# Pooling additions and half of the quarter sums on GpSimd, and attention spread anew over two blocks

## The chip, the cores and the metric

The kernel runs on one core of one Trainium2 chip. The metric is the device time of one execution in microseconds (us), from the start of the program on the core to its end; lower is better. Five engines work side by side, each through its own queue in order: TensorE (PE in the profile; its weight loads are PEld), VectorE (DVE), ScalarE (ACT), GpSimd (POOL) and SyncE (SP), which here only starts transfers. An engine whose next instruction waits for something does nothing else meanwhile.

## The reference

```python
# attention over pooled keys and values: 8 batches, 8 heads, 576 tokens, head size 64, pool 8
k_p = k.reshape(B, H, 72, 8, D).mean(axis=3)
v_p = v.reshape(B, H, 72, 8, D).mean(axis=3)
scores = scale * np.matmul(q, k_p.transpose(0, 1, 3, 2))
attn = softmax(scores)                       # max subtracted, sum + 1e-9
x = np.matmul(attn, v_p)                     # -> (4608, 512)
# the feed-forward part
h = x @ w_in                                 # (512, 2048)
g = h * np.clip(h + 3.0, 0.0, 6.0) / 6.0
out = g @ w_out                              # (2048, 512)
```

All is in float32. The kernel gets near that by splitting each factor of a large product into a rounded part and a remainder and making three products (rounded by rounded, rounded by remainder, remainder by rounded).

## The kernel before

**Blocks.** The 4608 tokens are cut into blocks of 512, 256, 384 and 384 tokens and then eight of 384. The first four are worked plainly. The last eight are taken in four pairs of 768 tokens, called super blocks below, numbers 0 to 3. In each, the feed-forward products are made by a fast scheme with seven products in place of eight (kinds 1 to 7): the four quarters of a factor are added to and subtracted from each other before and after.

**A super block** has two parts. The h part (`super_block`) makes h from x and the weights in 112 steps (products at L1134), adds kept results (L1098), applies the gate on ScalarE (L1090) and VectorE (L1092), and leaves g, whose quarters lie side by side in one tile per pair. The output part multiplies g by w_out. In super block 0 it is plain (`out_plain`, L1188), in 1 to 3 it goes by the seven kinds (`out_seven`, products at L1261). There, 28 steps follow each other, kinds in the order 1, 2, 4, 5, 6, 7, 3, four steps (m = 0 to 3) to a kind; each step has 18 products of 256 columns. Before each step a quarter of g is split by `split_g` into its rounded part (ScalarE, L1113) and the remainder (VectorE, L1115); there are three buffers for such parts, and a part is made two steps ahead. After the split for kind 1, `mix` makes quarter 0 minus 2 into 0 and 2 plus 3 into 2; after that for kind 4, 3 minus 0 into 3 and 1 minus 3 into 1 (L1218). A mix is an addition or subtraction of 128 x 768 numbers. The splits and mixes of m = 0, 1 and 2 for kind 1 already run during the h part.

**Attention for the next pair** is woven between the products of a super block by a pacer (`Paced`): so many steps per slot. A step is the scores of one 128-token tile for four heads (product, maximum on VectorE, four exponentials on ScalarE, sum and reciprocal on VectorE, and two products `a` and `ar` on GpSimd, L501 and L507), or the transposes of `a` (L572, L574) with the split of their result (L583, L585, L596, L598), or a product with the values (L646). `CUTS` says which share of a pair's attention steps goes to the h part of super blocks 0 to 3; the rest is spread over the first 48 of the 84 slots of the output part (in `out_plain`, over 66 slots), before x is combined for the next super block.

**Pooled values.** For each batch, `load_v` brings the values in ten transfers into ring buffers named vst (six of them, vr_l, for the last 8 pooled rows of each head), four buffers being shared with other tiles. `prep_v` then makes, three times per batch, three additions of halving width (512, 256 and 128 columns, L383) on VectorE, in place. `place_heads` (L395, L396) and `place_rest` (L409, L410) scale the sums, split them and put them into block-diagonal tiles `vhi`, `vlo` and `vrem`, the factors of the product with the values. At the first of them GpSimd clears two tiles (L374), which waits until the batch before last is no longer read.

**Order.** Up to some point in block 1 the order on each queue is written out by hand (`ORDER`). After it, a planner orders the instructions by its own estimates of their times. `after_mark` adds an edge that puts an instruction behind the last marked one of the same engine; marks are made for VectorE, ScalarE, and SyncE instructions of the feed-forward part, and for none of GpSimd's.

Of the kernel before, what the change touches and what calls it, by code (L numbers as in the profile page):

```python
# [13 lines left out]
ALU = mybir.AluOpType  # L14
# [31 lines left out]
SEVEN = (1, 2, 3)  # L46
MAKE = (range(8), (), (), ())
TURN = (0, 2, 4, 6, 7, 9, 10, 12)
CUTS = (.85, 0.85, 0.85, 0)
TAIL = 5  # L50
WSCALE = 2.0**8
GSCALE = WSCALE**-2
# [46 lines left out]
def attention_moe_kernel(  # L99
# [19 lines left out]
    nc = tc.nc  # L119
# [46 lines left out]
    def behind(ins, name):  # L166
        no_sync = mybir.DependencyInfo(mybir.DependencyClass.NoSync, mybir.DependencyReason.DATA)
        tc.add_manual_dep(ins, name, no_sync, reason="order")
# [14 lines left out]
    def after_mark():  # L183

        if len(window) == 2 and traced[-1].engine in marks:
            behind(traced[-1], marks[traced[-1].engine])
# [141 lines left out]
    class FirstValues:  # L328
# [19 lines left out]
        def place_heads(self):  # L348
            for h in range(2):
                rows = slice(h * D, (h + 1) * D)  # L350
                nc.scalar.mul(self.v32[rows, :, h * D : (h + 1) * D], self.ps[rows], 1.0 / POOL)
# [14 lines left out]
    def place_v(b):  # L366

        W[b] = (
            pool.tile([P, NPAIR, 2 * D], F32R, name="vhi", bufs=2),
            pool.tile([P, NPAIR, 2 * D], F32R, name="vlo", bufs=2),  # L370
            pool.tile([3 * REM, NG, 4 * D], F32R, name="vrem", bufs=2),
        )
        for w in W[b][:2]:
            nc.gpsimd.memset(w.bitcast(F32), 0.0)  # L374

    def prep_v(b, p):

        if p == 0 and b not in W:
            place_v(b)
        n = P if p < NPAIR else 3 * REM  # L380
        x, y = (vraw.pop((b, p + i))[:n, : POOL * D].rearrange("p (c n) -> p c n", c=2) for i in range(2))
        for w, a, c in ((4 * D, x, y), (2 * D, x, x[:, :, 2 * D :]), (D, x, x[:, :, D:])):
            nc.vector.tensor_tensor(out=x[:, :, :w], in0=a[:, :, :w], in1=c[:, :, :w], op=ALU.add)  # L383
            after_mark()
        if p < NPAIR:
            place_heads(b, x[:, :, :D], slice(p, p + 2))
        else:
            place_rest(b, x[:, :, :D])
# [16 lines left out]
    def place_rest(b, vs):  # L405
        lo = slice(REM, 2 * REM)
        for h in range(4):
            to, own = W[b][2][:, :, h * D : (h + 1) * D], mask[:NR, 2 + h : 3 + h]
            nc.scalar.mul(to, vs[:NR], own)  # L409
            nc.vector.scalar_tensor_tensor(  # L410
                out=to[lo],
                in0=vs[lo],
                scalar=own[lo],
                in1=to[lo].bitcast(F32),
                op0=ALU.mult,
                op1=ALU.subtract,
            )
# [238 lines left out]
    def side_steps(b):  # L656

        ks = [lambda p=p: load_k(b, p) for p in range(NPAIR)]
        ks += [lambda p=p: prep_k(b, p) for p in range(NPAIR)]
        vs = []  # L660
        n = NPAIR + NG
        for p in range(n):
            vs.append(lambda p=p: load_v(b, p))
            if p > 2 and p % 2:
                vs.append(lambda p=p: prep_v(b, p - 3))
        vs.append(lambda: prep_v(b, n - 2))
        return ks, vs
# [336 lines left out]
    def next_w2(n, x):  # L1004
        return chunk(first_of[n] + len(w_dram) + x).rearrange("p (k m c) -> p k m c", k=2, m=2)
# [198 lines left out]
    def out_seven(n, j, bank, parts, split_g, split_f, pairs, att, rest, last_h):  # L1204
        NT2, NM, W2 = HALF // P, NF // 4, DM // 2
        todo = [(o, m) for o in KINDS for m in range(NM)]
        n_tail = NT2 * 12
        paced, last = Paced(att, len(todo) * NT2 - n_tail), Paced([([], x) for x in rest], n_tail - NT2)
        rest.clear()
        sets = {"X": ["o2", "o1"], "Z": ["o0", "o3"], "V": ["h1", "h0"], "Y": ["o0", "o3"]}  # L1210
        on = {2: "Z", 1: "X", 4: "V", 5: "Y", 6: "X", 7: "X", 3: "Y"}
        first = (1, 2, 4, 5)
        src = {2: 1, 1: 0, 4: 3, 5: 2, 6: 3, 7: 0, 3: 1}
        ps, kept, made = {}, {}, [0]

        def mix(m, to, a, b, how):
            g = pairs[m]
            nc.vector.tensor_tensor(out=g[:, :, to], in0=g[:, :, a], in1=g[:, :, b], op=how)  # L1218

        def upto(x):  # L1220
            while made[0] <= x and made[0] < len(todo):
                o, m = todo[made[0]]
                split_g((o, m), pairs[m][:, :, src[o]])
                made[0] += 1
                if o == 1:
                    mix(m, 0, 0, 2, ALU.subtract)
                    mix(m, 2, 2, 3, ALU.add)
                elif o == 4:
                    mix(m, 3, 3, 0, ALU.subtract)
                    mix(m, 1, 1, 3, ALU.subtract)  # L1230

        def to_sbuf(o):
            c = late[1].tile([P, 2, HALF], F32, name="kept", tag="c", bufs=NC)
            kept[o] = c.rearrange("p a b -> p (a b)")
            for x, (lo, hi) in enumerate(((0, 2 * W2), (2 * W2, 3 * W2))):
                nc.scalar.copy(kept[o][:, lo:hi], ps[on[o]][x])

        def result(o, half, q, name):
            for x, (t0, t1) in enumerate(((0, 2), (2, 3))):
                c = kept[o][:, t0 * W2 : t1 * W2]  # L1240
                nc.vector.tensor_tensor(out=c, in0=ps[name][x], in1=c, op=ALU.add)
                at = starts[j] + half * HALF
                rows = out[at + t0 * P : at + t1 * P, q * W2 : (q + 1) * W2]
                nc.sync.dma_start(rows.rearrange("(t p) c -> p t c", p=P), c.rearrange("p (t c) -> p t c", c=W2))

        for x, (o, m) in enumerate(todo):
            upto(x + 2)
            w, t = next_w2(n, x), parts[o, m]
            name = on[o]
            if m == 0 and o in first:  # L1250
                ps[name] = [bank(sets[name], 0, 2 * W2), bank(sets[name], 1, W2)]
            for i in range(NT2):
                if x * NT2 + i < len(todo) * NT2 - n_tail:
                    paced.slot()
                else:
                    last.slot()
                to = ps[name][i // 2][:, i % 2 * W2 : (i % 2 + 1) * W2]
                begin = o in first and m == 0
                for k in range(2):
                    for y, (l, r) in enumerate(((0, 0), (0, 1), (1, 0))):  # L1260
                        nc.tensor.matmul(  # L1261
                            to,
                            t[:, l, k, i * P : (i + 1) * P],
                            w[:, k, r],
                            start=begin and k == 0 and y == 0 and i % 2 == 0,
                            stop=m == NM - 1 and k == 1 and y == 2,
                            skip_group_check=True,
                        )
                        if begin and k == 0 and y == 0:
                            behind(traced[-1], last_h if i % 2 == 0 else opened)  # L1270
                            opened = traced[-1].name
            if x * NT2 + NT2 >= len(todo) * NT2 - n_tail:
                paced.upto(len(paced.steps))
            if m < NM - 1:
                continue
            if o in (1, 4, 5, 6):
                to_sbuf(o)
            if o == 2:
                result(1, 0, 0, "Z")
            elif o == 7:  # L1280
                result(5, 1, 1, "X")
                result(4, 1, 0, "X")
            elif o == 3:
                result(6, 0, 1, "Y")
# [18 lines left out]
    a = [Step(first, f, 0, 2) for f in range(SPLIT)]  # L1303
# [33 lines left out]
    b = [Scores(t, g) for g in range(NG) for t in B]  # L1337
# [66 lines left out]
    def att_steps(j):  # L1404

        if j == 1:
            ks, _ = side_steps(1)
            return [([x], None) for x in ks[NPAIR:]] + [x[:2] for x in block_steps(1)]
        return [x[:2] for x in later_steps[j]]
# [106 lines left out]
    for n, j in enumerate(supers):  # L1516
        last = n == len(supers) - 1
        att = [] if last else att_steps(j + 2) + att_steps(j + 3)
        cut = int(CUTS[n] * len(att))
        super_block(n, j, att[:cut], att[cut:])  # L1520
# [46 lines left out]
```

## Time and profile before

| | us |
|---|---|
| median of three runs | 893.63 (892.76 to 893.68) |
| the profiled execution | 893.88 |
| its span in the profile | 892.1 |
| TensorE busy | 869.2 (97%) |
| VectorE busy | 665.9 (75%) |
| ScalarE busy | 553.6 (62%) |
| GpSimd busy | 83.6 (9%) |

The span is the time from the first to the last instruction of the execution. Places in it are given in us from its start. The super blocks lie at about 346 to 494 (output part from 423), 494 to 633 (from 566), 633 to 769 (from 704) and 769 to the end (from 828). A row of groups gives the line, the engine, the operation, what is written from what, the shapes and the count, then the busy time in us and the mean of one in ns, then the idle time before them and what ended it. A row of a time line gives start and length in us and, in brackets, the idle time before it and what ended that. The product time of TensorE is partly modelled: consecutive products overlap in the record.

### The profile page before, as it was taken

How to read it: one execution, taken by the hardware profiler on the slowest of the kernel's cores; microseconds unless marked ns; L12 is line 12 of the kernel's file. 1: busy time of each engine (PE TensorE's matmuls, PEld its weight loads, DVE VectorE, ACT ScalarE, POOL GpSimd, SP SyncE). 2: the span in 40 equal slices, each digit the busy share in tenths (PEclk: the TensorE clock that was granted, in tenths of full speed). 3: DMA queues.
4: the chain of work that ended last, by engine and by line, in shares of the span. 5: the costliest groups of instructions: out<-in, count | busy, mean ns of one | idle time of the engine just before them, and what ended most of it. 6: DMA issues, size and time to landing. Idle time of an engine off the chain costs nothing.

```text
span 892.1 us, 15646 instructions
## 1 busy us (share of the span) xinstructions
PE 869.2 (97%) x5360; PEld 812.3 (91%) x5360; DVE 665.9 (75%) x1340; ACT 553.6 (62%) x1515; POOL 83.6 (9%) x168
## 2 busy tenths in 40 slices
PE   7899999999999999999999999999999999999998
PEld 6788888988989998998888999999999999999998
DVE  6999864567877785869788688897597877466664
ACT  5998766655656655778344688665577746355442
POOL 4100002110211100102000101100100200000000
PEclk9999999999999999999999999999999999999999
DMA  9970205995425234996587968877976777877873
GB/s 294 392 293 1 72 24 192 360 327 167 130 67 160 71 129 135 368 315 225 180 271 239 383 218 295 265 239 236 331 250 213 226 233 240 275 253 238 266 264 132
DMA packets 124654, 200.00 MB, mean 224 GB/s; under 512 B 13216, under 2 KB 81056, under 8 KB 124576
## 3 DMA queue, kind: packets, MB, share of 16 engines
q1 hardware_dynamic: 124432, 199.00, 67.8%
q8 instruction: 43, 0.70, 0.3%
q14 instruction: 35, 0.29, 0.1%
q10 hardware_dynamic: 144, 0.00, 0.0%
HBM read 158.08 MB, written 40.89 MB: 223 GB/s over the span
## 4 chain that ended last, share of the span: by engine, by line
PE 80%; DVE 8%; DMA 5%; ACT 4%; issue 2%; SPq 1%; POOL 0%; DVEq 0%; ACTq 0%; POOLq 0%
PE psx L1134 22%; PE psx L1261 19%; PE pso L872 12%; PE psh L841 12%; PE psx L1188 7%; PE psa L646 3%; PE psa L463 3%; ACT e L472 2%; PE psa L572 1%; DMA raw<-w_in_l 1%; DMA raw<-w_out_l 1%; DMA wd<-wq 1%; DVE vst L383 1%; DMA wsFalse<-wd 1%; DVE wq L939 1%
## 5 line engine op out<-in xcount | busy, mean ns | idle before, releaser
L1134 PE MATMUL psx<-x,wsFalse 128*128 128x384 f32 x768 | 151.8, 341 | 1.7 <-DVE g L1098 0.8
L841 PE MATMUL psh<-xhi,w 128*128 128x384 f32 (+2 forms) x520 | 145.9, 340 | 0.5 <-DVE g L853 0.4
L1134 PEld LDWEIGHTS psx<-x,wsFalse 128*128 128x128 f32 x768 | 133.6, 188 | 3.2 <-ACT c L1107 1.3
L1113 ACT CAST part<-g 128x768 fp32r<-128x768 f32 x100 | 83.3, 836 | 85.0 <-PE psx L1261 65.8
L1115 DVE TENSOR_TENSOR part<-g,part 128x768 fp32r<-128x768 f32 x100 | 95.2, 955 | 46.5 <-ACT part L1113 46.1
L872 PE MATMUL pso<-w,ghi 128*128 128x512 f32 x384 | 120.7, 398 | 0.4 <-ACT o L877 0.4
L1134 PE MATMUL psx<-x,wsTrue 128*128 128x384 f32 x576 | 115.8, 342 | 2.4 <-DMA wsTrue<-wd 2.3
L1261 PE MATMUL psx<-wsFalse,part 128*128 128x256 f32 x864 | 108.3, 282 | 1.5 <-DVE part L1115 1.1
L1261 PEld LDWEIGHTS psx<-wsFalse,part 128*128 128x128 f32 x864 | 105.2, 189 | 2.3 <-DVE part L1115 1.3
L1134 PEld LDWEIGHTS psx<-x,wsTrue 128*128 128x128 f32 x576 | 99.6, 188 | 3.1 <-DVE g L1092 3.1
L841 PEld LDWEIGHTS psh<-xhi,w 128*128 128x128 f32 x520 | 93.2, 188 | 8.2 <-DVE g L853 1.1
L472 ACT ACTIVATE e<-psa,mx 128x72 f32<-128x72 f32 x256 | 78.6, 324 | 23.7 <-DVE mx L467 22.4
L841 PE MATMUL psh<-xlo,w 128*128 128x384 f32 (+2 forms) x260 | 87.1, 336 | 0.0
L501 POOL TENSOR_TENSOR a<-e,sm 128x256 f32<-128x256 f32 x60 | 41.0, 683 | 478.3 <-DVE sm L490 377.9
L1261 PE MATMUL psx<-wsTrue,part 128*128 128x256 f32 x648 | 81.3, 283 | 0.0
L1261 PEld LDWEIGHTS psx<-wsTrue,part 128*128 128x128 f32 x648 | 79.3, 191 | 0.2 <-DVE part L1115 0.2
L872 PEld LDWEIGHTS pso<-w,ghi 128*128 128x128 f32 x384 | 69.1, 188 | 11.2 <-ACT o L877 0.7
L1090 ACT ACTIVATE r<-g,small 128x384 f32<-128x384 f32 x96 | 58.8, 621 | 28.4 <-DVE g L1098 28.0
L872 PE MATMUL pso<-w,glo 128*128 128x512 f32 x192 | 74.4, 399 | 0.0
L1098 DVE TENSOR_TENSOR g<-psx,c 128x384 f32<-128x384 f32 x96 | 52.3, 553 | 28.7 <-PE psx L1134 20.6
L1107 ACT COPY c<-psx 128x384 f32<-128x384 f32 x96 | 45.0, 485 | 28.5 <-PE psx L1134 28.1
L1092 DVE SCALAR_TENSOR_TENSOR g<-r,g 128x384 f32<-128x384 f32 x96 | 54.5, 576 | 9.7 <-ACT r L1090 9.2
(139 smaller groups left out, 1473.2 us busy)
## 6 DMA issues: line engine op xcount, KB each, us to landing
wsFalse<-wd SPq DMA_DIRECT2D x64, 512.0 KB, 4.6
wsTrue<-wd SPq DMA_DIRECT2D x48, 512.0 KB, 4.9
wsFalse<-w2d SPq DMA_DIRECT2D x31, 512.0 KB, 5.0
wsFalse<-w2t SPq DMA_DIRECT2D x27, 512.0 KB, 5.0
wsTrue<-w2d SPq DMA_DIRECT2D x21, 512.0 KB, 5.0
wsTrue<-w2t SPq DMA_DIRECT2D x21, 512.0 KB, 4.9
raw<-w_in_l SPq DMA_DIRECT2D x16, 512.0 KB, 8.6
raw<-w_out_l SPq DMA_DIRECT2D x16, 512.0 KB, 9.2
```

Of the source, the lines that this page charges most:

```text
L472: nc.scalar.activation(self.e[:, h], self.ps[:, h], AF.Exp, bias=self.mx[:, h : h + 1], accum_out=self.sm[:, h : h + 1])
L841: nc.tensor.matmul(self.ps, l[f][:, c, :], r[:, c, :], start=c == 0 and i == 0, stop=c == NCC - 1 and i == 2)
L872: nc.tensor.matmul(pos, l, r, start=f == 0 and i == 0, stop=f == NF - 1 and i == 2)
L1090: nc.scalar.activation(r, src, AF.Relu, bias=half_low, scale=GSCALE / (6.0 * WSCALE))
L1092: nc.vector.scalar_tensor_tensor(out=g_of[i][:, k], in0=r, scalar=GSCALE, in1=src, op0=ALU.min, op1=ALU.mult)
L1098: nc.vector.tensor_tensor(out=g_of[i][:, k], in0=ps, in1=kept, op=ALU.add)
L1107: nc.scalar.copy(c, ps)
L1113: nc.scalar.copy(t[:, 0], src)
L1115: nc.vector.tensor_tensor(out=t[:, 1], in0=src, in1=t[:, 0].bitcast(F32), op=ALU.subtract)
L1134: nc.tensor.matmul(ps, w[:, l, c * P : (c + 1) * P], t[:, r, c], start=o in (1, 2, 5) and c == 0 and k == 0, stop=c == 1 and k == 2, skip_ ...
L1188: nc.tensor.matmul(to, l, w[:, qs, r], start=f == 0 and k == 0, stop=end and k == 2)
L1261: nc.tensor.matmul(to, t[:, l, k, i * P : (i + 1) * P], w[:, k, r], start=begin and k == 0 and y == 0 and i % 2 == 0, stop=m == NM - 1 and ...
```

## The change

The three additions of `prep_v` go to GpSimd for batches 3 to 7 (batches 1 and 2 lie before or in the stretch ordered by hand, or use another function). `after_mark` is still called after each, but since GpSimd has no mark, it adds no edge. In `out_seven`, the mixes into quarters 1 and 2 go to GpSimd, those into 0 and 3 stay on VectorE. `CUTS` puts 65% in place of 85% of the next pair's attention into the h parts of super blocks 1 and 2, and so 35% in place of 15% into their output parts.

```diff
-CUTS = (.85, 0.85, 0.85, 0)
+CUTS = (.85, .65, .65, 0)
...
         for w, a, c in ((4 * D, x, y), (2 * D, x, x[:, :, 2 * D :]), (D, x, x[:, :, D:])):
-            nc.vector.tensor_tensor(out=x[:, :, :w], in0=a[:, :, :w], in1=c[:, :, :w], op=ALU.add)
+            engine = nc.gpsimd if b > 2 else nc.vector
+            engine.tensor_tensor(out=x[:, :, :w], in0=a[:, :, :w], in1=c[:, :, :w], op=ALU.add)
             after_mark()
...
         def mix(m, to, a, b, how):
             g = pairs[m]
-            nc.vector.tensor_tensor(out=g[:, :, to], in0=g[:, :, a], in1=g[:, :, b], op=how)
+            engine = nc.gpsimd if to in (1, 2) else nc.vector
+            engine.tensor_tensor(out=g[:, :, to], in0=g[:, :, a], in1=g[:, :, b], op=how)
```

## The prediction

> **What bounds the kernel now.** I read the page first: the busy shares and the chain that ended last.
>
> ```profile
> span 892.1 us, 15646 instructions
> PE 869.2 (97%) x5360; PEld 812.3 (91%) x5360; DVE 665.9 (75%) x1340; ACT 553.6 (62%) x1515; POOL 83.6 (9%) x168
> PE 80%; DVE 8%; DMA 5%; ACT 4%; issue 2%; SPq 1%; POOL 0%; DVEq 0%; ACTq 0%; POOLq 0%
> ```
>
> TensorE is the bound: it is busy 97% and carries 80% of the chain. The change takes no product away, so all that it can win is time in which PE stands still for another engine. VectorE's 8% of the chain is the candidate. The span is 892.1; the profiled execution took 893.88, so 1.8 us lie around the span, and it stands 0.25 above the median of the three runs, 893.63.
>
> Next, busy time in chosen stretches: length of the stretch, then busy time (instructions) of PE, PEld, DVE, ACT, POOL. I take the super blocks alone: of the moved work only batch 3's nine additions lie before them.
>
> ```profile
> 361.00:400.00 39.00, 39.00 (x236) 38.86 (x235) 32.30 (x77) 30.07 (x97) 4.16 (x10) 1.00 1.01 347
> 400.00:424.00 24.00, 22.69 (x139) 21.51 (x139) 20.75 (x58) 20.53 (x82) 6.16 (x11) 1.00 0.69 220
> 545.00:585.00 40.00, 37.81 (x259) 36.14 (x259) 34.98 (x75) 28.21 (x82) 5.62 (x12) 1.00 0.82 265
> 695.00:708.00 13.00, 12.41 (x86) 11.85 (x85) 10.82 (x30) 10.44 (x40) 3.99 (x8) 1.00 0.68 215
> 828.00:888.00 60.00, 60.00 (x504) 59.83 (x504) 36.70 (x45) 25.04 (x35) 0.00 (x0) 1.00 0.68 227
> ```
>
> PE is without work for 1.31 us at the end of the first 768-token block's h part, for 2.19 us where the second block passes from h to its output part, for 0.59 us at that place of the third block; in the stretches between, such as the first and the last row here, it is full. DVE is at 83 to 87% in just those three. The granted clock is 1.00 throughout. Then who PE waited for (total, times, longest), from the waits after 270 us (the one for the first weight chunk, near 356, is left out, since no edit touches it):
>
> ```profile
> PE psa L463 <- DVE arem L598: 1.3, 3, 0.9
> PE psx L1261 <- DVE part L1115: 1.1, 1, 1.1
> PE psx L1134 <- DVE g L1098: 0.8, 1, 0.8
> ```
>
> All three are DVE results, 3.2 of the 4.1 us. The time lines of PE and of DVE at two of these places say why DVE is late:
>
> ```profile
> 416.48 0.69 DVE L383 TENSOR_TENSOR vst<-vst 96x512 f32<-96x512 f32 x1 [0.81 <-DMA vst<-vr_l]
> ...
> 572.31 0.69 DVE L383 TENSOR_TENSOR vst<-vst 96x512 f32<-96x512 f32 x1 [3.57 <-DMA vst<-vr_l]
> ...
> 417.74 0.76 PE L463 MATMUL psa<-kbd,qt 128*128 128x144 f32 x4 [0.90 <-DVE arem L598]
> ...
> 581.63 2.04 PE L1261 MATMUL psx<-wsFalse,part 128*128 128x256 f32 x15 [1.07 <-DVE part L1115]
> ```
>
> The pooling add stands at the head of DVE's queue and waits for its values, 0.81 and 3.57 us, with everything else of DVE behind it; PE's 0.90 us pause ends 1.3 us after the first of these adds starts, its 1.07 us pause 9.3 us after the second.
>
> **The change part by part.** The groups concerned (busy us, mean ns, idle before):
>
> ```profile
> L383 DVE TENSOR_TENSOR vst<-vst 128x512 f32<-128x512 f32 (+5 forms) x54 | 26.2, 486 | 4.7 <-DMA vst<-vr_l 4.4
> L1218 DVE TENSOR_TENSOR g<-g 128x768 f32<-128x768 f32 x48 | 45.4, 953 | 0.4
> L1115 DVE TENSOR_TENSOR part<-g,part 128x768 fp32r<-128x768 f32 x100 | 95.2, 955 | 46.5 <-ACT part L1113 46.1
> L357 POOL TENSOR_TENSOR stage<-stage 32x512 f32<-32x512 f32 x1 | 1.3, 1252 | 8.1 <-DMA stage<-vr_l 8.1
> L357 POOL TENSOR_TENSOR stage<-stage 32x256 f32<-32x256 f32 x1 | 0.7, 715 | 0.1
> L501 POOL TENSOR_TENSOR a<-e,sm 128x256 f32<-128x256 f32 x60 | 41.0, 683 | 478.3 <-DVE sm L490 377.9 <-ACT e L472 30.5 <-ACT wq L945 22.6
> ```
>
> *Off DVE.* Six batches make the 54 adds; five of them (3 to 7) move, 45 x 0.486 = 21.9 us. Two of four mixes per pair move, 24 x 0.953 = 22.9 us. Together 44.8 of 665.9 us.
>
> *Onto POOL.* POOL's own two-tensor adds took 1.252 and 0.715 us: 0.537 per 256 columns. From these I estimate 0.45 us at 128 and 1.79 at 768 columns (lower end: DVE's 0.95; upper end: 2.5, twice the one at 512). An add group is 1.25 + 0.72 + 0.45 = 2.4 us instead of DVE's 3 x 0.486 = 1.46; 15 groups make 36 us, the mixes 43 us. POOL goes from 84 to some 163 us, 18% of the span. So throughput is no question; latency is. A batch's values come some 1 us later per group. A mix has time: the quarter that kind 5 reads is made eight or more steps ahead, and a step is 18 products of 0.119 us (504 in 60.00 us) = 2.14 us, so 17 us cover 1.8.
>
> *The shared read port.* What DVE wins by an add that leaves it can be lost where POOL's add holds DVE up. The trace has it:
>
> ```profile
> 406.56 0.61 POOL L501 TENSOR_TENSOR a<-e,sm 128x256 f32<-128x256 f32 x1 [0.49 <-DVE sm L490]
> 407.13 1.00 POOL L507 TENSOR_TENSOR ar<-e,sm 128x64 f32<-128x64 f32 x1
> ...
> 406.69 1.30 DVE L1038 TENSOR_TENSOR x<-x,x 128x768 fp32r<-128x768 f32 x1 [0.30 <-ACT x L1037]
> ...
> 420.12 1.31 POOL L501 TENSOR_TENSOR a<-e,sm 128x256 f32<-128x256 f32 x1 [7.64 <-DVE sm L490]
> ```
>
> A DVE add with both inputs in SBUF, started 0.13 us behind POOL's, took 1.30 where its like takes 0.95 (L1115's row); POOL's next, behind that one, took 1.00, its 0.61 us instruction at another place 1.31. They exclude each other. A mix on POOL can therefore hold DVE for up to 1.79 us, against the 0.95 it took as DVE's own. Where DVE is packed I count the moved adds as no gain at all (bounds per mix: +0.95 won, 0.84 lost); what stays is the *wait for the load*, which no longer stands in DVE's queue.
>
> The Trainium skill says the same as a rule (SBUF — State Buffer, "Who interferes with whom": a DVE instruction with two SBUF inputs and a GpSimd instruction that reads SBUF take the port as an exclusive lock). The rule speaks against the change, and the trace agrees, 1.30 against 0.95 us. Without the rule, DVE's freed 44.8 us would take back all 4.1 us of pauses, times the 1.3 worked out below: 5.3 us, 888.3 for the median; with it stands the sum below, 890.7.
>
> *Waits that move.* The 0.81 and 3.57 us waits go to POOL's queue. Behind them there stand `a`/`ar` products of attention, memsets and mixes. Who waits for `a` are PE's transposes, and PE runs in order:
>
> ```profile
> L572 PE MATMUL psa<-ident,a 128*128 128x128 f32 x128 | 24.7, 273 | 1.2 <-POOL a L501 0.7 <-issue 0.5
> ...
> 560.88 0.75 POOL L501 TENSOR_TENSOR a<-e,sm 128x256 f32<-128x256 f32 x1 [0.43 <-DVE sm L490]
> ...
> 561.69 0.44 PE L572 MATMUL psa<-ident,a 128*128 128x128 f32 x2
> ```
>
> Today this costs PE 0.7 us in all 60; at the tightest place PE starts 0.06 us after `a` is done. At the 416 us wait the next `a` comes at 420.12, 3.6 us after the values landed, so nothing is behind it. I charge 0.5 us for late `a`s (0 to 4). The ring slots of the values come free some 1 us later, so SP's next loads too; SP runs five weight chunks ahead, which covers it: 0. The adds also lose their ordering edge, since POOL never gets a mark; the planner may put them elsewhere. I charge nothing for it, and it widens the range.
>
> *The spreading.* CUTS 0.85 to 0.65 for blocks two and three moves 20 points of the next pair's attention from h to output parts. Nothing is added. What the output part has free is shown by block four, which has no attention there:
>
> ```profile
> 843.10 0.96 DVE L1218 TENSOR_TENSOR g<-g 128x768 f32<-128x768 f32 x1
> 844.24 0.96 DVE L1115 TENSOR_TENSOR part<-g,part 128x768 fp32r<-128x768 f32 x1 [0.18 <-ACT part L1113]
> 845.11 0.95 DVE L1218 TENSOR_TENSOR g<-g 128x768 f32<-128x768 f32 x1
> ...
> 843.36 0.84 ACT L1113 CAST part<-g 128x768 fp32r<-128x768 f32 x1 [1.29 <-PE psx L1261]
> ```
>
> The cast starts when PE gives up a buffer (843.36) and the part is whole at 845.20, 1.84 us later; PE needs it two steps after the cast's start, 4.28 us: 2.4 us of slack. In the steps of kinds 1 and 4 DVE now does 0.955 + 2 x 0.953 = 2.86 us per 2.14; with one mix gone 1.91, which fits. So the output part can take in more attention, and the packed end of h gets lighter. I charge 0.5 us (0 to 3) for PE meeting attention there that isn't ready.
>
> *Sum.* Of the pauses 1.31, 2.19 and 0.59 I take 1.0, 1.8 and 0.3 back (0 to all): 3.1 us. PE's busy time hides part of a pause, since the last product before it is drawn 0.27 us long and spaced 0.1 (L572's mean; a step's spacing above): by about 1.3 times, the real gain is 4.0. Less 0.5 + 0.5 for POOL and the output parts: -3.0. 893.88 - 3.0 = 890.9 profiled, 890.7 for the median.
>
> **The rivals.**
> - *Hidden anyway.* The lock gives back what DVE wins, the same load is waited for by `vrem` and then by PE's product with it, so PE pauses as long at the next instruction. For it: the chain needs those values in any case. Against it: PE's 1.1 us wait names a part, not the values. Gain under 1 us: 893.3.
> - *POOL's queue becomes late (slower).* In 494 to 633 POOL had 15 us; one batch (7.3) and eight mixes (14.3) make it 36 of 139, 26%. Some 42 `a`s come after 270 us; 42 x 0.26 x 0.9 (half a mix) = 9.8 us of lateness, of which a third gets past the slack, 3.3 us. It decides once `a`'s slack is below 0.9 us, as at 561. With 1 us of gain left: 896.2.
> - *The port in series (slower).* If POOL's mix gets the port after every DVE add, a step of kind 4 needs 0.955 + 0.953 + 1.79 = 3.70 us per 2.14: 1.56 late each, 6.2 in four steps, less 2.4 slack = 3.8 in each of three blocks: 893.9 - 3 + 11.4 = 902. Against it: DVE's instructions start before the last one ends (845.11 against 845.20), so with a backlog DVE keeps the port and POOL waits, as its 1.31 us shows.
>
> **How the numbers follow.** Forecast 0.52, own range 888.0 to 892.5; hidden 0.22; POOL late 0.17; series 0.09. The measurement tells 0.2%, 1.8 us, from no change: 891.8 to 895.4 is "same". Faster: 0.47 of the forecast's 0.52 and 0.03 of the hidden case, 0.50. Same: 0.05 of the forecast, 0.18 of the hidden case and 0.03 of POOL late, 0.26. Slower: the rest, 0.24. The low end takes in all 4.1 us of pauses at 1.3 and no charge, with a little of replanning: 887.0. The high end takes in "POOL late": 896.5, with a tenth above it.
>
> **What would show it.** Right: no DVE wait on the values' load; PE idle in 400 to 424 and around the second block's change of part under half of 3.5 us; POOL near 160 us busy; mixes on POOL near 1.8 us, longer where DVE runs; DVE near 620 us or more by what the lock adds. Wrong: PE's transposes waiting for POOL by more than 2 us, PE waiting for parts in the output parts, or pauses where none stood because the planner dealt the work anew.

## The result and the profile after

The changed kernel takes 907.88 us (median of four, 903.04 to 909.77), the kernel before on the same chip 893.65 (892.76 to 895.72). The ratio is 1.0158, 95% interval 1.0136 to 1.0180: slower by 14 us. The forecast was 890.7 with a range up to 896.5, so the sign and the range are both wrong. The execution whose profile follows took 909.77 us.

The page of the kernel after: the span, busy times and the chain that ended last.

```profile
span 908.0 us, 15599 instructions
PE 876.8 (97%) x5360; PEld 817.6 (90%) x5360; DVE 666.8 (73%) x1271; ACT 552.5 (61%) x1515; POOL 180.0 (20%) x237
PE 73%; DVE 12%; DMA 5%; ACT 5%; issue 2%; POOL 2%; SPq 1%; ACTq 0%; DVEq 0%; POOLq 0%
```

VectorE has 69 instructions less (1271 for 1340) and is busy as long as before, 666.8 us for 665.9. All that left it came back as longer instructions, and its share of the chain rose from 8% to 12%. The groups of the kernel after show which instructions grew. All line numbers from the middle of the code on are one or two above those of before: L1116 is the remainder of a split, L1093 the gate, L1099 the addition of kept results, L1220 the mix, L384 the pooling addition. The first two rows are those of the gate and of the addition of kept results in the kernel before.

```profile
L1092 DVE SCALAR_TENSOR_TENSOR g<-r,g 128x384 f32<-128x384 f32 x96 | 54.5, 576 | 9.7 <-ACT r L1090 9.2
L1098 DVE TENSOR_TENSOR g<-psx,c 128x384 f32<-128x384 f32 x96 | 52.3, 553 | 28.7 <-PE psx L1134 20.6 <-ACT c L1107 6.0 <-issue 0.9
...
L1116 DVE TENSOR_TENSOR part<-g,part 128x768 fp32r<-128x768 f32 x100 | 107.0, 1072 | 43.6 <-ACT part L1114 41.8
L1093 DVE SCALAR_TENSOR_TENSOR g<-r,g 128x384 f32<-128x384 f32 x96 | 64.2, 678 | 12.3 <-ACT r L1091 12.1
L1099 DVE TENSOR_TENSOR g<-psx,c 128x384 f32<-128x384 f32 x96 | 52.6, 554 | 36.1 <-PE psx L1135 23.2
L1220 POOL TENSOR_TENSOR g<-g 128x768 f32<-128x768 f32 x24 | 52.4, 2185 | 159.1 <-DVE g L1220 147.8
L384 POOL TENSOR_TENSOR vst<-vst 128x512 f32<-128x512 f32 (+5 forms) x45 | 43.2, 960 | 42.3 <-DMA vst<-v_l 22.8 <-DVE wq L945 8.2 <-DMA vst<-vr_l 7.9
```

The split's remainder went from 955 to 1072 ns and the gate from 576 to 678. Both read two operands from SBUF, where the kernel keeps its tiles. L1099, which reads one operand from PSUM, where its products land, stayed at 554 (553 before). The growth sits in single instructions: the median remainder still takes 958 ns (957 before), the longest 2591 (964 before). A mix on GpSimd took 2.19 us in the mean.

The time lines of GpSimd and VectorE in the last output part show the exclusion at work, instruction by instruction (start, length).

```profile
861.32 0.41 DVE L1243 TENSOR_TENSOR kept<-psx,kept 128x256 f32<-128x256 f32 x1
861.54 1.85 POOL L1220 TENSOR_TENSOR g<-g 128x768 f32<-128x768 f32 x1 [0.96 <-DVE g L1220]
861.65 2.56 DVE L1116 TENSOR_TENSOR part<-g,part 128x768 fp32r<-128x768 f32 x1
```

GpSimd starts at 861.54, while VectorE runs an instruction that reads PSUM; VectorE's next one, due at 861.65, then takes 2.56 us in place of 0.95. The mix takes 1.85 us, and VectorE loses 1.61 us here.

Where TensorE stood still, from the stretches of the kernel after (length, then busy time of PE, PEld, DVE, ACT, POOL, then the granted clock, which is 1.00 at full speed), and from its waits (total, times, longest):

```profile
400.00:428.00 28.00, 26.00 (x143) 24.52 (x143) 24.62 (x60) 21.70 (x83) 12.39 (x18) 0.89 0.67 208
545.00:585.00 40.00, 37.19 (x246) 36.34 (x245) 29.23 (x54) 25.50 (x80) 17.66 (x21) 0.96 0.83 268
585.00:605.00 20.00, 15.84 (x117) 15.37 (x116) 18.30 (x24) 8.74 (x25) 11.19 (x8) 0.91 0.71 227
840.00:900.00 60.00, 58.50 (x480) 57.72 (x479) 39.55 (x41) 25.83 (x36) 11.78 (x5) 1.00 0.71 232
```

The stretch from 585 to 605 in the kernel before:

```profile
585.00:605.00 20.00, 20.00 (x167) 20.00 (x166) 19.35 (x25) 11.77 (x18) 0.00 (x0) 1.00 0.72 231
```

The waits of the kernel after:

```profile
PE psx L1263 <- DVE part L1116: 5.9, 6, 3.8
PE psa L464 <- ACT e L473: 1.8, 1, 1.8
PE psa L647 <- DVE alo L586: 1.4, 3, 1.0
PE psa L573 <- POOL a L502: 0.7, 1, 0.7
```

The last output part, full before, has 1.5 us of pauses; 585 to 605, also full before, has 4.2. TensorE's waits for parts went from 1.1 to 5.9 us. Its waits for GpSimd's `a` stayed at 0.7, so TensorE did not wait longer for that. The pooled sums did come later: ScalarE's waits for them before `vhi` rose from 1.8 us to 10.6.

The largest pause, from the time lines of VectorE, GpSimd and TensorE of the kernel after:

```profile
591.72 0.95 DVE L1116 TENSOR_TENSOR part<-g,part 128x768 fp32r<-128x768 f32 x1
591.87 2.50 POOL L1220 TENSOR_TENSOR g<-g 128x768 f32<-128x768 f32 x1 [0.90 <-DVE g L1220]
592.70 1.82 DVE L411 SCALAR_TENSOR_TENSOR vrem<-vst,small,vrem 32x128 fp32r<-32x128 f32 x1
...
597.05 0.96 DVE L1220 TENSOR_TENSOR g<-g 128x768 f32<-128x768 f32 x1
597.93 0.95 DVE L1116 TENSOR_TENSOR part<-g,part 128x768 fp32r<-128x768 f32 x1
...
598.94 3.68 PE L1263 MATMUL psx<-wsTrue,part 128*128 128x256 f32 x18 [3.80 <-DVE part L1116]
```

And line L411 as a whole in that kernel (shortest, median and longest in ns):

```profile
L411 DVE SCALAR_TENSOR_TENSOR vrem<-vst,small,vrem x24: 333/336/1825, 215.2 to 682.7; 32x128 fp32r<-32x128 f32 x24
```

Two things meet here. VectorE makes no part from 592.67 to 597.93, because work for `vrem` and `kept`, a remainder of the next pair's attention and a mix stand ahead of it: that is the order that the planner dealt. And one of those, L411, takes 1.82 us where the median is 0.336: GpSimd's mix of 591.87 to 594.37 lies over it. Which of the two the 14 us come from is the question for the experiments.

A third loss comes on top. The granted clock was 1.00 in the stretches shown of the kernel before; here it is 0.89, 0.96 and 0.91 in three of them. In steps of one us:

```profile
564.00:565.00 1.00, 0.00 (x0) 0.00 (x0) 0.36 (x2) 1.00 (x8) 0.00 (x0) 1.00 0.77 260
565.00:566.00 1.00, 0.99 (x5) 0.99 (x6) 0.97 (x4) 0.65 (x3) 0.48 (x1) 0.74 0.89 307
566.00:567.00 1.00, 1.00 (x4) 1.00 (x4) 0.61 (x2) 0.92 (x4) 0.38 (x2) 0.50 0.42 158
...
568.00:569.00 1.00, 1.00 (x5) 1.00 (x4) 0.98 (x3) 0.53 (x1) 0.00 (x0) 0.55 0.01 4
```

```profile
565.01 0.91 PE L464 MATMUL psa<-kbd,qt 128*128 128x144 f32 x4 [1.81 <-ACT e L473]
```

After a pause of 1.81 us TensorE runs at half clock for about 3.4 us. There are three such places in this execution, behind the pauses at 420, 565 and 599 (at 420 it lasts nearly 7 us). From the clocks of the three stretches above they take, as an estimate, 28 x 0.11 = 3.1, 40 x 0.04 = 1.6 and 20 x 0.09 = 1.8 us, 6.5 together. This execution is the slowest of the four; their mean clock is 0.9945, against 0.9984 in 24 executions of the kernel before, so in the mean it is an estimated 0.0039 x 908 = 3.5 us, a quarter of the loss.

The pause at 565 itself shows both causes and a late sum. GpSimd's mix of 557.33 to 559.89 lies over VectorE's gate at 558.11, which takes 2.20 us; ScalarE waits 2.56 us for the addition behind that gate, and then 0.56 us for a pooled sum that GpSimd made behind the same mix.

### The profile page after: what moved, and what is told of

It is laid out like the page before. It is cut to its first block, busy times and chain, and to the rows that moved or that the text cites. A ratio compares the mean times of both kernels' runs of the same rounds, so it can differ in the third digit from the quotient of the medians.

```text
span 908.0 us, 15599 instructions
## 1 busy us (share of the span) xinstructions
PE 876.8 (97%) x5360; PEld 817.6 (90%) x5360; DVE 666.8 (73%) x1271; ACT 552.5 (61%) x1515; POOL 180.0 (20%) x237
## 4 chain that ended last, share of the span: by engine, by line
PE 73%; DVE 12%; DMA 5%; ACT 5%; issue 2%; POOL 2%; SPq 1%; ACTq 0%; DVEq 0%; POOLq 0%
PE psx L1135 19%; PE psx L1263 14%; PE pso L873 13%; PE psh L842 12%; PE psx L1189 7%; PE psa L647 4%; PE psa L464 3%; ACT e L473 2%; DVE part L1116 2%; DVE g L1093 1%; DMA wsTrue<-wd 1%; DVE g L1220 1%; DMA raw<-w_in_l 1%; DMA vst<-v_l 1%; POOL vst L384 1%
## 5 line engine op out<-in xcount | busy, mean ns | idle before, releaser
L1116 DVE TENSOR_TENSOR part<-g,part 128x768 fp32r<-128x768 f32 x100 | 107.0, 1072 | 43.6 <-ACT part L1114 41.8
L1263 PE MATMUL psx<-wsFalse,part 128*128 128x256 f32 x864 | 110.2, 283 | 2.2 <-DVE part L1116 1.7
L1263 PE MATMUL psx<-wsTrue,part 128*128 128x256 f32 x648 | 83.9, 287 | 4.3 <-DVE part L1116 4.2
L1220 POOL TENSOR_TENSOR g<-g 128x768 f32<-128x768 f32 x24 | 52.4, 2185 | 159.1 <-DVE g L1220 147.8
L1099 DVE TENSOR_TENSOR g<-psx,c 128x384 f32<-128x384 f32 x96 | 52.6, 554 | 36.1 <-PE psx L1135 23.2
L1093 DVE SCALAR_TENSOR_TENSOR g<-r,g 128x384 f32<-128x384 f32 x96 | 64.2, 678 | 12.3 <-ACT r L1091 12.1
```

Source lines behind the costliest of these rows:

```text
L1093: nc.vector.scalar_tensor_tensor(out=g_of[i][:, k], in0=r, scalar=GSCALE, in1=src, op0=ALU.min, op1=ALU.mult)
L1099: nc.vector.tensor_tensor(out=g_of[i][:, k], in0=ps, in1=kept, op=ALU.add)
L1116: nc.vector.tensor_tensor(out=t[:, 1], in0=src, in1=t[:, 0].bitcast(F32), op=ALU.subtract)
L1220: engine.tensor_tensor(out=g[:, :, to], in0=g[:, :, a], in1=g[:, :, b], op=how)
L1263: nc.tensor.matmul(to, t[:, l, k, i * P : (i + 1) * P], w[:, k, r], start=begin and k == 0 and y == 0 and i % 2 == 0, stop=m == NM - 1 and ...
```

## The experiments

The theories. *Lock*: GpSimd's reads hold VectorE up by as much as it was relieved, and it costs what TensorE then waits. *Order*: the planner dealt the work anew, and the new order is worse. The runs of this section were made in three sets on three chips, each set with the kernel before beside it (medians 894.1, 893.74 and 894.38). A time is given with its ratio to the kernel before in its set; what is compared across sets are ratios, times 894 us.

**The three parts apart.** Only the pooling additions on GpSimd:

```diff
-            nc.vector.tensor_tensor(out=x[:, :, :w], in0=a[:, :, :w], in1=c[:, :, :w], op=ALU.add)
+            engine = nc.gpsimd if b > 2 else nc.vector
+            engine.tensor_tensor(out=x[:, :, :w], in0=a[:, :, :w], in1=c[:, :, :w], op=ALU.add)
```

> Only the pooling additions of batches 3 to 7 go to GpSimd; mixes and shares as before. Three theories. Lock: GpSimd's two-input adds and VectorE's two-input instructions exclude each other, and the add takes 1.5 us where VectorE took 0.68; values come late and VectorE's work on them (vlo, vrem) gets longer than 0.29 and 0.34 us; TensorE then pauses near 421 us for 1 to 2 us and perhaps runs at half clock after it: 895 to 899 us. Spreading: all the loss is the new shares, so nothing is lost here: 891 to 894 us. Planner: the order dealt anew costs by chance, any of the edits alone shows some of it: 893 to 900, with pauses at places that have no moved add near them.

Measured: 899.5 us, ratio 1.0055 (1.0038 to 1.0071), +4.9 us.

Only the mixes:

```diff
-            nc.vector.tensor_tensor(out=g[:, :, to], in0=g[:, :, a], in1=g[:, :, b], op=how)
+            engine = nc.gpsimd if to in (1, 2) else nc.vector
+            engine.tensor_tensor(out=g[:, :, to], in0=g[:, :, a], in1=g[:, :, b], op=how)
```

> Only the mixes into quarters 1 and 2 go to GpSimd. Lock: the mixes on GpSimd take 1.85 us alone and up to 2.6 where VectorE works, VectorE's remainders (0.955 us alone) take 1.07 or more on average, and TensorE waits for parts in the steps of kind 4 of super blocks 1 to 3, some 1.5 us in each, as in the whole change near 864 to 872 us: 897 to 900 us, and a half-clock stretch adds 1.7 us where a pause is long enough. Spreading: 893 to 894 us. Planner: no such pauses at the kind-4 steps.

Measured: 901.99 us, ratio 1.0087 (1.0060 to 1.0114), +7.8 us.

Only the spreading:

```diff
-CUTS = (.85, 0.85, 0.85, 0)
+CUTS = (.85, .65, .65, 0)
```

> Only the shares of attention are changed (0.65 in place of 0.85 in super blocks 1 and 2). Lock: no new work on GpSimd, so no loss: 891 to 895 us, VectorE's remainders at 0.955 us. Spreading: TensorE waits in the output parts for attention that isn't ready and for parts that stand behind attention on VectorE, 4 to 8 us: 898 to 903 us.

Measured: 893.1 us, ratio 0.9993 (0.9977 to 1.0008): no difference.

Additions and mixes together, without the spreading (the two edits above):

> Additions and mixes on GpSimd, shares as before. Lock: the sum of the two single edits, or more where a mix and an add fall together: 899 to 905 us, VectorE's busy time no less than before although 45 us of work have left it. Spreading: 893 to 895 us.

Measured: 908.49 us, ratio 1.0157 (1.0131 to 1.0183), +14.0 us. The whole loss is in the two moves, 4.9 and 7.8 us by each alone; the spreading adds nothing. In all these runs the planner dealt the order anew, so none of them parts the two theories.

**The order held.** The same moves, with the instructions of TensorE, ScalarE, VectorE and SyncE chained to the order of the kernel before (GpSimd's order is left to the planner):

```diff
+    for name, part in PIN.items():
...
+        mine = [rest[n] for n in order if n in rest and rest[n].engine == getattr(mybir.EngineType, name)]
+        for x, y in zip(mine, mine[1:]):
+            behind(y, x.name)
```

> Additions and mixes on GpSimd as in e4, but TensorE, ScalarE, VectorE and SyncE keep the order of the kernel before, instruction by instruction (the moved ones left out of VectorE's). Lock: the loss is there all the same, 903 to 912 us, VectorE's two-input groups longer by 5 to 20% and its groups with one input in PSUM not. Planner: with the old order the loss is gone, 892 to 896 us.

Measured: 896.29 us, ratio 1.0021 (1.0003 to 1.0038), +1.9 us. The same instructions on the same engines in the old order lose 12.2 us less than in the new one (1.0157 less 1.0021). Its loss now shows one clean chain, in the time lines of GpSimd, VectorE and TensorE (L1488 is the mix, L1307 an addition of two SBUF operands, L867 the remainder that TensorE's L732 has to wait for):

```profile
555.69 1.83 POOL L1488 TENSOR_TENSOR g<-g 128x768 f32<-128x768 f32 x1 [4.50 <-DVE g L1488]
...
555.99 2.35 DVE L1307 TENSOR_TENSOR x<-x,x 128x768 fp32r<-128x768 f32 x1
...
558.45 0.29 DVE L867 TENSOR_TENSOR arem<-psa,arem 32x128 fp32r<-32x128 f32 x1
...
558.88 0.73 PE L732 MATMUL psa<-kbd,qt 128*128 128x144 f32 x4 [1.92 <-DVE arem L867]
```

GpSimd's mix makes VectorE's addition 2.35 us long, and TensorE's pause of 1.92 us ends with the remainder behind it. The same place in the kernel before:

```profile
557.51 0.73 PE L463 MATMUL psa<-kbd,qt 128*128 128x144 f32 x4 [0.16 <-DVE arem L598]
```

The other half: nothing moved, with TensorE's, ScalarE's and SyncE's order that of the run with both moves. VectorE's is not chained and is near that order, but not the same; the ordering edge of the additions of batches 3 to 7 is left out, as it is in the changed kernel:

```diff
-            after_mark()
+            if b <= 2:
+                after_mark()
```

> Nothing is on GpSimd that wasn't there before, but TensorE, ScalarE and SyncE go in the order that the planner made for e4, and VectorE nearly so. Lock: little is lost, 893 to 898 us, and VectorE's remainders take 0.955 to 0.97 us. Planner: the loss of e4 is in the order: 904 to 909 us.

Measured: 905.23 us, ratio 1.0118 (1.0081 to 1.0156), +10.5 us. By itself this number would say that the order alone costs 10 us. The time line says otherwise (L580 is the pooling addition, L699 the product `a`):

```profile
562.92 0.69 DVE L580 TENSOR_TENSOR vst<-vst 96x512 f32<-96x512 f32 x1 [3.12 <-DMA wsTrue<-w2d]
...
564.58 0.44 PE L770 MATMUL psa<-ident,a 128*128 128x128 f32 x2 [3.98 <-POOL a L699]
```

With the additions still on VectorE, one of them stands 3.12 us at the head of its queue (the profile names a transfer of weights as what ended the wait), and TensorE's pause behind it is 3.98 us. So this run shows the old fault in a worse place together with the new order, and can't price the order by itself.

**The lock alone.** The kernel before, with its own order chained and nothing moved; GpSimd makes 24 more additions of 128x768, with `g` read and a spare tile written, for which nobody waits:

```diff
+        def extra(m, q):
+            g = pairs[m]
+            nc.gpsimd.tensor_tensor(out=idle_to, in0=g[:, :, q], in1=g[:, :, q], op=ALU.add)
```

> The kernel before in its own order on all engines, with all mixes on VectorE, and 24 more GpSimd additions of 128 x 768 that nobody waits for: each reads a quarter of g that a mix has just made and writes a spare tile. So GpSimd reads what it reads in e2 and no work leaves VectorE. Lock: this alone costs what e2 costs or more: 900 to 910 us, VectorE's remainders 1.04 us or more on average. If lateness of the moved results were the cause (a queue on GpSimd, a longer add), nothing is lost here: 893 to 895 us.

Measured: 904.81 us, ratio 1.0124 (1.0099 to 1.0148), +11.1 us. And the control, with two columns read and three memsets of 640 columns in place of each addition:

```diff
+            nc.gpsimd.tensor_tensor(out=idle_to[:, :, :1], in0=g[:, :, q, :1], in1=g[:, :, q, :1], op=ALU.add)
+            for _ in range(3):
+                nc.gpsimd.memset(idle_to[:, :, : 320], 0.0)
```

> As e9, but GpSimd is kept busy as long by writing alone: after a read of two columns three memsets of 640 columns into the spare tile. Lock on reading: no loss, 893 to 895 us, VectorE's remainders 0.955 us. If any work on GpSimd slows VectorE (its writes too, or memory as such): 900 us or more, as e9.

Measured: 894.54 us, ratio 1.0005 (0.9990 to 1.0019). The busy times from the pages of the two, the run with reads first, and the groups of the run with reads (L1318 splits, L1421 mixes, L1427 is the idle addition):

```profile
PE 874.4 (97%) x5360; PEld 814.8 (90%) x5360; DVE 688.6 (76%) x1340; ACT 555.4 (61%) x1515; POOL 128.7 (14%) x192
```

```profile
PE 870.2 (98%) x5360; PEld 813.1 (91%) x5360; DVE 665.7 (75%) x1340; ACT 554.9 (62%) x1515; POOL 149.0 (17%) x264
```

```profile
L1318 DVE TENSOR_TENSOR part<-g,part 128x768 fp32r<-128x768 f32 x100 | 102.3, 1028 | 38.4 <-ACT part L1316 38.1
L1421 DVE TENSOR_TENSOR g<-g 128x768 f32<-128x768 f32 x48 | 57.8, 1211 | 0.4
...
L1427 POOL TENSOR_TENSOR spare<-g 128x768 f32<-128x768 f32 x24 | 43.8, 1825 | 195.8 <-DVE g L1421 195.7
```

GpSimd is busier in the second run (149.0 for 128.7 us), yet VectorE is untouched there (665.7 for 665.9) and grew by 22.7 us in the first: 0.95 us for each idle addition, and the kernel grew by half as much. So it is reading on GpSimd that costs. The splits and mixes of the first take 1028 and 1211 ns for 955 and 953. Nothing waits for the idle additions, so lateness of their results has no part in it. The second run also says that chaining the order changes nothing by itself.

**The moves without the lock.** The additions moved but cut to one column on GpSimd, in the new order and in the old one. This leaves out nearly all of the moved pooling sums and quarter sums:

```diff
+            w = 1 if b > 2 else w
...
+            n = 1 if to in (1, 2) else HALF
+            engine.tensor_tensor(out=g[:, :, to, :n], in0=g[:, :, a, :n], in1=g[:, :, b, :n], op=how)
```

> The order that the planner made for the moved additions, kept on TensorE, ScalarE, VectorE and SyncE, while the moved additions are cut to one column each on GpSimd. This leaves out of the computation nearly all of the moved pooling sums of batches 3 to 7 and of the moved quarter sums, so VectorE is freed of 44.8 us and GpSimd reads next to nothing. If the new order is good for a VectorE that is really freed and only the lock spoils it, it comes out faster than before: 887 to 892 us. If the order is poor whatever VectorE does, it stays slow: 900 us or more. VectorE busy about 621 us (665.9 less 44.8), L1116 near 955 ns a part in both.

Measured: 891.86 us, ratio 0.9973 (0.9963 to 0.9984), -2.4 us.

> The order of the kernel before on TensorE, ScalarE, VectorE and SyncE, with the moved additions cut to one column each on GpSimd; the same sums are left out as in the run before. It is the most that the move could give were the additions free on GpSimd. If the lock has taken back what the move gives (the same order with whole additions took 896.3 us), it comes out at 887 to 891 us, so the lock costs 5 to 9 us in the old order. If VectorE's load is not what the pauses come from, 893 to 894 us.

Measured: 887.37 us, ratio 0.9930 (0.9916 to 0.9945), -6.3 us. The busy times of the old order with one column and with whole additions, each from its page:

```profile
PE 868.3 (98%) x5360; PEld 812.9 (92%) x5360; DVE 631.4 (71%) x1271; ACT 553.6 (63%) x1515; POOL 104.1 (12%) x237
```

```profile
PE 871.9 (97%) x5360; PEld 814.2 (91%) x5360; DVE 664.0 (74%) x1271; ACT 555.0 (62%) x1515; POOL 176.9 (20%) x237
```

The lock gives VectorE back 32.6 us (664.0 less 631.4) of the 34.5 that it is relieved of (665.9 less 631.4). The four runs make a table, in us against the kernel before (the new order is that of the run with both moves; GpSimd's own order was left to the planner in all four):

| | one column (no lock to speak of) | whole additions | the lock costs |
|---|---|---|---|
| old order | -6.3 | +1.9 | 8.1 |
| new order | -2.4 | +14.0 | 16.4 |
| the new order costs | 3.8 | 12.2 | |

One column also makes the moved additions short (267 and 399 ns in the mean), so the last column holds whatever a late result costs besides the lock; in the old order with whole additions none of TensorE's waits listed from 270 us on names GpSimd.

Neither theory is the whole. The new order is good enough for a VectorE that is really freed, faster than before even. Without the lock it costs 3.8 us, of which its time line shows two pauses of TensorE that the old order does not have:

```profile
349.08 6.57 PE L1397 MATMUL psx<-x,wsFalse 128*128 128x384 f32 x36 [1.27 <-ACT o L1140]
561.70 2.38 PE L1397 MATMUL psx<-x,wsFalse 128*128 128x384 f32 x12 [1.64 <-ACT c L1370]
```

Under the lock the same order has no slack where VectorE turns out late, and the two together cost 8.3 us more than the sum of each alone (16.4 less 8.1; from the four intervals uncertain by some 3 us). Some 3.6 of the 8.3 us are half clock, an estimate from the mean clocks: 0.9930 in the new order with whole additions, 0.9977, 0.9982 and 0.9990 in the other three. A likely reason for the rest, argued and not shown: the order was dealt for a VectorE without the moved instructions, and the lock made VectorE as heavy as before. That the planner would have dealt a better order had it been told of the lock was not tried.

**Smaller moves in the old order.** Only the pooling additions:

> Only the pooling additions of batches 3 to 7 on GpSimd, in the order of the kernel before. With the planner's new order the same move took 899.5 us against 894.1. If most of that was the order: 891 to 895 us, and if the waits for vr loads that VectorE loses are worth the 3 us that were forecast, 891. If it was the lock: 898 to 900 us.

Measured: 893.1 us, ratio 0.9992 (0.9979 to 1.0005): no difference. The same move in the planner's order had lost 4.9 us. The mixes are then worth a loss of 2.6 us in the old order (1.0021 less 0.9992), if the two add up.

Only the additions of the 96-row pair, the ones that stood at the head of VectorE's queue:

```diff
+            engine = nc.gpsimd if b > 2 and p == NPAIR else nc.vector
+            engine.tensor_tensor(out=x[:, :, :w], in0=a[:, :, :w], in1=c[:, :, :w], op=ALU.add)
```

> Only the additions of the 96-row pair in batches 3 to 7 on GpSimd, those that stand at the head of VectorE's queue and wait for the vr load, in the order of the kernel before. They are 15 instructions, so the lock takes little. If the waits at the head of the queue cause the pauses of TensorE, as was forecast: 890 to 892 us. If they are hidden by TensorE's backlog: 893 to 894 us. If the lock decides even here: over 895 us.

Measured: 891.44 us, ratio 0.9969 (0.9954 to 0.9983), -2.8 us: faster than both kernels, with nothing left out, and with the old order held; what the planner would make of this edit was not run. The thirty other additions thus bring no gain of their own: with them it is 0.7 us, without them 2.8. Its profile at the places of the prediction, in the time line, the groups and the stretches (L652 is the pooling addition):

```profile
416.32 2.75 POOL L652 TENSOR_TENSOR vst<-vst 96x512 f32<-96x512 f32 x3 [4.24 <-DMA vst<-vr_l]
419.08 0.61 POOL L770 TENSOR_TENSOR a<-e,sm 128x256 f32<-128x256 f32 x1
```

```profile
L652 DVE TENSOR_TENSOR vst<-vst 128x512 f32<-128x512 f32 (+5 forms) x39 | 21.2, 543 | 0.2
```

```profile
400.00:424.00 24.00, 23.01 (x141) 21.89 (x140) 21.70 (x57) 21.03 (x81) 8.93 (x15) 1.00 0.75 230
545.00:585.00 40.00, 38.83 (x275) 37.46 (x274) 36.52 (x73) 28.46 (x80) 8.57 (x13) 1.00 0.85 277
```

GpSimd now waits 4.24 us for the values, and the next `a` starts behind the additions without a wait; VectorE's idle time before its pooling additions is 0.2 us in place of 4.7. TensorE's pauses fall from 1.31 to 0.99 us and from 2.19 to 1.17, and its 1.1 us wait for a part is gone. That is 1.3 us of the 2.8 (interval 1.5 to 4.1); the rest isn't visible in pauses: TensorE's busy time for the same products is 867.6 us in place of 869.2.

## Why the prediction was wrong, point by point

- *What bounds the kernel*: right. VectorE's lateness makes TensorE pause. (That VectorE is at 83 to 87% "in just those three" stretches is a misreading: the first row, where TensorE is full, has 32.30 of 39.00 us, 83% as well. The waits mark the places, not the load.) With VectorE relieved and no lock, 6.3 us came off; the most the prediction gave for taking back every pause was 5.3.
- *Off DVE*: 44.8 us was the sum of the groups. With one column on GpSimd VectorE's groups add up to 43.2 us less (723.6 to 680.4), but its busy time fell by 34.5 only, since busy time counts overlapping records once (in the prediction's rows a part starts at 844.24 for 0.96 us and the next instruction at 845.11, 0.09 us before its end). "DVE near 620" was too low by that before any lock.
- *Onto POOL*: a mix of 1.79 us was right for a mix alone (1.83 to 1.85) and short for the mean, 2.19, as GpSimd waits for VectorE too. GpSimd is busy 180 us in place of 163. TensorE's wait for `a` stayed at 0.7 us, so "POOL's queue becomes late" is refuted as it was put, through `a`, and the 0.5 us charged for it was not needed. What came late were pooled sums that ScalarE waits for, as at 562, and for these there was no term.
- *The shared read port*: the failed step that the forecast rests on. "I count the moved adds as no gain at all" was right of VectorE's busy time (32.6 given back of 34.5) and wrong of the kernel's time. A gain comes as a fraction of a microsecond per instruction; the lock comes in pieces of up to 1.6 us (a remainder of 2.59 us for 0.96) on whatever two-operand instruction is next, and where TensorE waits for that one it pauses. In the old order the moves come out at +1.9 us, not -3.0: the term was mis-sized by 5 us. The gain from the wait for the load, forecast as what stays, is there: 2.8 us in the run with the 96-row additions alone.
- *The adds lose their ordering edge*: "I charge nothing for it, and it widens the range". This step failed most. The planner dealt the order anew on all engines, which costs 12.2 us under the lock. "Pauses where none stood because the planner dealt the work anew" was on the list of what would make the prediction wrong, and it had no price. The range was widened for it at the low end only, 888.3 to 887.0; its high end, 896.5, was set by another rival. Of the way from the forecast -3.0 to the measured +14.0 us, 4.9 are the step above and 12.2 this one. Which share the lost edge has, against the moves themselves, was not separated.
- *The spreading*: 0.5 us charged, 0 measured.
- *The port in series* (0.09, 902 us): its place was right, parts that TensorE waits for in the output parts. What was said against it, that VectorE keeps the port in a backlog, is refuted at 861.54, where GpSimd takes the port during a VectorE instruction that reads PSUM. Its price of 3.8 us a block was met once (3.80 at 598.94), together with the order. That 902 lay nearest of all to the measured time was luck in part: most of the loss is the order, which this rival did not have.
- *Hidden anyway*: refuted. With only the additions that wait for the load taken off VectorE, the kernel gains 2.8 us (1.5 to 4.1), where this rival allowed under 1.
- *Sum*: the factor 1.3 does not follow from 0.27 and 0.1 us. Their difference, 0.17 us for each of three pauses, is 0.5 on 3.1 us, a factor of 1.16. With one column in the old order TensorE's time without work fell by 5.7 us (892.1 less 869.2 before, 885.5 less 868.3 in that run) and the span by 6.6, which is 1.16 too.
- *The clock*: no term for it. The pauses cost an estimated 3.5 us more in the mean by the half clock behind them.

## What to carry to other kernels

Work moved from VectorE to GpSimd relieves VectorE only where GpSimd doesn't read SBUF while VectorE reads two operands from it; count each GpSimd read as up to nearly its own length laid on VectorE's next such instruction (1.6 of 1.85 us at the worst here, 0.95 in the mean of the idle additions), and look which engine waits for that one. Move what waits, not what is merely long: fifteen small additions that stood at the head of a queue were worth 2.8 us in the old order, all sixty-nine moved instructions a loss of 1.9. Where a planner orders the work, hold the old order once to see what the edit does by itself, since the new order may be the larger part of a loss (12.2 of 14.0 us here).

## What the runs showed of the hardware that was not expected

- GpSimd's *reads* hold up VectorE's instructions with two operands from SBUF, its writes do not: 24 idle additions lengthened VectorE by 22.7 us, 72 memsets by nothing, at more GpSimd time. The Trainium skill (SBUF — State Buffer, "Who interferes with whom") states that rule, and these two runs agree with it.
- TensorE's clock fell to half for about 3.4 us behind a single pause of 1.81 us (at 565, above) and for longer behind three short ones, from the time line of the kernel after:

```profile
420.60 0.33 PE L647 MATMUL psa<-ahi,vhi 128*128 128x192 f32 x1 [1.01 <-DVE alo L586]
421.94 0.40 PE L647 MATMUL psa<-ahi,vhi 128*128 128x192 f32 x1 [0.79 <-ACT e L473]
422.96 0.74 PE L647 MATMUL psa<-arem,vrem 96*128 96x192 f32 x2 [0.20 <-DVE arem L599]
```

A longer pause in the kernel before left it at 1.00 (time line, and the stretch around it, where the clock is the last column but two):

```profile
358.70 3.56 PE L1134 MATMUL psx<-x,wsTrue 128*128 128x384 f32 x19 [2.34 <-DMA wsTrue<-wd]
```

```profile
350.00:362.00 12.00, 9.66 (x57) 9.37 (x56) 5.35 (x12) 7.20 (x21) 0.86 (x2) 1.00 1.01 339
```

The run with idle reads has a pause of 2.05 us at the same product, and there the clock is 0.50 from 359 to 362. So the length of a pause alone does not decide; what does was not settled.
